# Block-sparse attention and an expert router on one core: masks multiplied on GpSimd in some units, sums read from PSUM, squares on ScalarE, ranks in 16 bits, one branch at the end

## The chip, the cores and the metric

The kernel runs on one core of a Trainium2 chip. The core has five engines with a queue each: TensorE (PE in the profile, its weight loads PEld), VectorE (DVE), ScalarE (ACT), GpSimd (POOL) and SyncE (SP), which issues most of the transfers. The metric is the device time of one execution in microseconds (us).

## The reference, cut to what matters

Four batches of eight heads attend over 768 tokens with a mask of 32 x 32 blocks: a block sees its neighbours, the first and the last block, and three blocks drawn at random. The result, 3072 rows of 512, goes to a router that sends each row to the one of eight experts whose embedding it is closest to in angle, and the expert's two matmuls are scaled by the gate.

```python
# attention: q, k, v are (4, 8, 768, 64)
scores = scale * np.matmul(q, k.transpose(0, 1, 3, 2))
mask = np.abs(blk_i - blk_j) <= 1
mask = mask | (blk_i == 0) | (blk_j == 0) | (blk_i == n_blocks - 1) | (blk_j == n_blocks - 1)
for qb in range(n_blocks):
    for kb in sampled_blocks[qb]:
        mask[qb * block:(qb + 1) * block, kb * block:(kb + 1) * block] = True
scores = np.where(mask, scores, -1000000000.0)
attn = np.exp(scores - np.max(scores, axis=-1, keepdims=True))
attn = attn / (np.sum(attn, axis=-1, keepdims=True) + 1e-09)
attn_out = np.matmul(attn, v)
x = attn_out.transpose(0, 2, 1, 3).reshape(3072, 512)
# router: w1 is (8, 512, 1024), w2 is (8, 1024, 512)
xn = x / (np.linalg.norm(x, axis=-1, keepdims=True) + 1e-06)
en = expert_emb / (np.linalg.norm(expert_emb, axis=-1, keepdims=True) + 1e-06)
logits = xn @ en.T / tau
expert_idx = np.argmax(logits, axis=1)
probs = np.exp(logits - logits.max(-1, keepdims=True))
probs /= probs.sum(-1, keepdims=True) + 1e-09
gate_w = probs[np.arange(N), expert_idx]
for e in range(E):
    mask = expert_idx == e
    h = np.maximum(x[mask] @ w1[e], 0.0)
    out[mask] = gate_w[mask, None] * (h @ w2[e])
```

## The kernel before

The attention is cut into 16 pairs of heads (g), each pair into two halves of 384 queries (qh, a half has the number w), each half into six units of 128 keys (kc): 192 units, numbered u. For a unit, score_fast adds the mask and the scores up in PSUM (both heads and both halves of the keys side by side, 64 x 64 each, so four matmuls for the mask and four for the scores) and ScalarE takes the exponential. Masked places get a large negative number from the mask's matmul, a product of two 16-bit tables of blocks, so that the exponential is zero.

```python
def score_fast(k, u):

    nc = k.nc
    g, qh, kc = u // (2 * NC), u // NC % 2, u % NC
    kt, qt = k.turned[g]
    ps = k.big.tile([P, 2, 512], F32, name="sc", tag="big")
    queries = slice(qh * HALF, (qh + 1) * HALF)
    quarters = [(h, r, slice(kc * P + D * r, kc * P + D * (r + 1))) for r in range(2) for h in range(2)]
    for rows, cols, first in ((k.kmask, k.qmask, True), (kt, qt, False)):
        for h, r, keys in quarters:
            nc.tensor.matmul(ps[D * r:D * (r + 1), h, 0:HALF], lhsT=rows[D * h:D * (h + 1), keys],
                             rhs=cols[D * h:D * (h + 1), queries], start=first, stop=not first)
    e = k.ep.tile([P, 2, HALF], F32, name="e", tag="e")
    k.exps = nc.scalar.activation(e, ps[:, :, 0:HALF], ACT.Exp, scale=SCALE)
    k.es[u] = e


def attend_fast(k, u):
    nc = k.nc
    g, qh, kc = u // (2 * NC), u // NC % 2, u % NC
    e, v = k.es[u], k.loaded[g][2]
    if kc == 0:
        k.av = k.acc.tile([P, 2, 512], F32, name="av", tag="av")
        k.first = e
    elif kc == 1:
        k.esum = k.sp.tile([P, 2, HALF], F32, name="esum", tag="esum")
        with k.tc.issue_after(k.summed.ins if u > NC else k.exps.ins):
            k.summed = nc.vector.tensor_tensor(out=k.esum, in0=k.first, in1=e, op=ALU.add)
    else:
        k.summed = nc.vector.tensor_tensor(out=k.esum, in0=k.esum, in1=e, op=ALU.add)
    for r in range(2):
        for h in range(2):
            nc.tensor.matmul(k.av[D * h:D * (h + 1), r, 0:HALF], lhsT=v[D * r:D * (r + 1), h, kc, :],
                             rhs=e[D * r:D * (r + 1), h, :], start=(kc == 0), stop=(kc == NC - 1))
    if kc == NC - 1:
        part = k.sp.tile([P, HALF], F32, name="part", tag="part")
        nc.scalar.copy(out=part, in_=k.av[:, 1, 0:HALF])
        at = k.sp.tile([P, HALF], F32, name="at", tag="at")
        k.summed = nc.vector.tensor_tensor(out=at, in0=k.av[:, 0, 0:HALF], in1=part, op=ALU.add)
        k.done[u // NC] = (at, k.esum)
```

At the end of a half, settle turns the result back into rows, sums the exponentials of each row with matmuls by ones, and divides. The squares of the rows (for the router's norm) are taken on GpSimd, and those of the last half on ScalarE.

```python
    # settle(k, w): at is turned back into PSUM (rows) by matmuls, and then
    for t in range(NQ):
        for h in range(2):
            for r in range(2):
                for s in range(2):
                    cols = slice(t * P + D * s, t * P + D * (s + 1))
                    nc.tensor.matmul(sums[D * s:D * (s + 1), t, h, r:r + 1], lhsT=esum[D * r:D * (r + 1), h, cols],
                                     rhs=k.ones[D * r:D * (r + 1), 0:1], start=True, stop=True)
    den = k.dens[:, w, :]
    nc.vector.reduce_sum(out=den.rearrange("p (t h) -> p t h", t=NQ), in_=sums, axis=AX.X)
    nc.vector.tensor_scalar(out=den, in0=den, scalar1=1e-9, scalar2=None, op0=ALU.add)
    # ... (1 / den times rows gives x, and the partial logits, both on VectorE)


def squares(k, w):

    nc = k.nc
    b, j, qh = w // (2 * NPAIR), w // 2 % NPAIR, w % 2
    chunks = slice(qh * NQ, (qh + 1) * NQ)
    x = k.x[b][:, chunks, j, 0:P]
    sq = k.sp.tile([P, NQ, P], F32, name="sq", tag="sq", bufs=1)
    nc.gpsimd.tensor_tensor(out=sq, in0=x, in1=x, op=ALU.mult)
    width = P // 2
    while width:
        out = sq[:, :, 0:width] if width > 1 else k.nsq[b][:, chunks, j:j + 1]
        k.squared = nc.gpsimd.tensor_tensor(out=out, in0=sq[:, :, 0:width], in1=sq[:, :, width:2 * width],
                                            op=ALU.add).ins
        width //= 2
```

The loop over the units, in which scores run two units ahead of attend:

```python
    for u in range(units):
        # ...
        if u % NC == 3 and NC < u < units - 2 * NC:
            settle(n, u // NC - 1)
        if u % NC == 4 and NC < u < units - 2 * NC:
            squares(n, u // NC - 1)
        # ... (routing, ranks and early dispatch of a finished batch, by a plan)
        steps = [partial(attend_fast, n, u)] + ([partial(score_fast, n, u + 2)] if u + 2 < units else [])
        for step in reversed(steps) if u % NC == 0 else steps:
            step()
        # ... (the next pair's keys and queries are turned in units 0 and 1 of a pair)
```

The rank of a row in its expert, by triangular and full matrices of ones (k.before, k.ones, fp32):

```python
    oh = k.oh[:, b * NC:(b + 1) * NC, :]
    ps = two_banks(k, "rk")[:, 0]
    rk = ps[:, 0:NC * E].rearrange("p (c e) -> p c e", e=E)
    nc.tensor.matmul(rk, lhsT=k.before, rhs=oh, start=True, stop=False)
    nc.tensor.matmul(rk, lhsT=k.ones, rhs=k.seen[:, b * NC:(b + 1) * NC, :], start=False, stop=True)
    nc.tensor.matmul(ps[:, NC * E:(NC + 1) * E], lhsT=k.ones, rhs=k.seen[:, (b + 1) * NC, :], start=True, stop=True)
```

The expert tiles have 128 rows of one expert. Five (NE) are made from the first two batches while attention still runs, the later ones when all rows are known. Late tiles number NL = 24 at most, of which NU = 19 are always run and the others if k.used, the number that the routing asks for, is larger. Weights are fetched up to two tiles ahead into three sets of buffers, rows two tiles ahead, and the rows of the next tile are turned (prepare) before the second matmul of the tile before it.

```python
def fetch(k, i):

    if i + 2 < NE + NL and i + 2 != NE:
        fetch_rows(k, i + 2)
    need = [(t, at) for t in range(NE + NL) for at in parts(t)]
    begin = [t for t, _ in need].index(i)
    for t, at in need[k.loads:begin + 3]:
        for _ in fetch_weights(k, t, at):
            pass


def expert_tile(k, i, meanwhile=None, then=None):
    # ... hp: two halves of 4 x 4 matmuls by w1, relu into h, then
    if i + 1 < NE + NL:
        prepare(k, i + 1)
    # ... yp: 8 matmuls by w2; finish: y = gate * yp on VectorE, scattered to the output by GpSimd


# end of expert_tiles
    for i in range(NE + NU):
        if i + 2 == NE:
            for _ in between:
                pass
        fetch(n, i)
        # ... (expert_tile, or mixed_tile for two halves of 64 rows of two experts)
    used = n.nc.values_load(n.used[0:1, 0:1], min_val=0, max_val=NL)
    with ExitStack() as more:
        for i in range(NU, NL):
            more.enter_context(n.tc.If(used > i))
            n.scattered = None
            fetch(n, NE + i)
            expert_tile(n, NE + i)
```

Rows of late tiles come from memory by four indirect transfers that GpSimd issues, and VectorE turns them (from fetch_rows and prepare, cut):

```python
            for g in range(NG):
                k.nc.gpsimd.indirect_dma_start(
                    out=x[:, g], out_offset=None, in_=quarters,
                    in_offset=bass.IndirectOffsetOnAxis(ap=k.quarter[:, g, t:t + 1], axis=0),
                    bounds_check=quarters.shape[0] - 1, oob_is_err=False,
                )
# ...
    with k.tc.issue_after(k.relu):
        nc.vector.transpose(out=turned.rearrange("p d (g t) -> p d g t", g=NG),
                            in_=x[:, :, 0:P].rearrange("p g (t d) -> p d g t", d=ND))
```

At the very end a second branch asks whether all row sums were in a safe range (count_good); if not, exact computes everything again with the row's maximum taken off first.

```python
    fast(n)
    good = n.nc.values_load(n.good[0:1, 0:1], min_val=0, max_val=N * H)
    with tc.If(good < N * H):
        exact(n)
```

## Time and profile before

| | |
|---|---|
| time, median of 3 | 699.31 us (699.29 to 699.33) |
| span of the profiled execution | 697.6 us |
| exponentials on ScalarE, 192 | 155.5 us, 810 ns each |
| matmuls of scores, 1536 records | 164.4 us busy |
| matmuls of attend, 1536 records | 160.7 us busy |
| mask matmuls, 768 | 73.7 us busy, 323 ns each |
| additions of exponentials on VectorE, 128 and 32 | 128.8 and 31.1 us |
| squares on GpSimd, 31 and 217 instructions | 28.5 us and some 114 us |
| memory read and written | 147.66 and 16.07 MB |

Matmuls overlap: the time of one record is from its start to its end, and several are under way at once, so a stage is read from the distances between starts. A group's busy time is the union of its records. In a list in order of time, records of one kind that follow each other are merged, with their number behind an x; in brackets stands how long the engine had been idle and what ended that.

### The profile page before, as it was taken

Reading aid. Unit: us, or ns where it says so; the run is one execution under the profiler, and the core shown is the slowest. Engines: PE = TensorE matmul, PEld = TensorE weight load, DVE = VectorE, ACT = ScalarE, POOL = GpSimd, SP = SyncE. Lnnn points to the kernel's source line nnn. Section 1 sums busy time; section 2 is a strip of 40 time slices with the busy share of each in tenths; the row PEclk is TensorE's granted clock in tenths of the full one; section 3 lists DMA queues with packets and bytes.
Section 4 is the critical chain, followed back from the end, with each engine's and each line's share of the span. In section 5 each row is a group of like instructions: output and inputs, shape, how many; then the busy total and the mean of one; then the engine's idle time right before and its main releaser. Section 6 shows DMA issues by size and latency. Waiting matters only on the chain.

```text
span 697.6 us, 19415 instructions
## 1 busy us (share of the span) xinstructions
PE 682.9 (98%) x8237; PEld 453.5 (65%) x8237; DVE 344.4 (49%) x733; ACT 188.4 (27%) x266; POOL 295.6 (42%) x450
## 2 busy tenths in 40 slices
PE   9999999999999999999999999999999999999992
PEld 4677777555555557557767677666576755667770
DVE  6887778777788888765671111211121111211120
ACT  5555555555555555553100000000100000000000
POOL 1355466544774468545402244323342243323430
PEclk9999999999999999999999999999999999999997
DMA  7733444575226769652999889998899998999990
GB/s 123 130 62 50 55 70 70 130 145 118 55 43 161 138 160 195 222 172 94 341 406 369 339 303 341 357 350 302 297 409 403 405 372 310 420 390 419 359 342 25
DMA packets 172650, 164.87 MB, mean 236 GB/s; under 512 B 129340, under 2 KB 129340, under 8 KB 169478
## 3 DMA queue, kind: packets, MB, share of 16 engines
q1 hardware_dynamic: 165734, 149.86, 68.0%
q0 software_dynamic: 5216, 13.43, 5.3%
q8 instruction: 68, 1.11, 0.7%
q10 hardware_dynamic: 1600, 0.20, 0.2%
q14 instruction: 32, 0.26, 0.1%
HBM read 147.66 MB, written 16.07 MB: 235 GB/s over the span
## 4 chain that ended last, share of the span: by engine, by line
PE 96%; DMA 1%; issue 1%; DVE 0%; POOL 0%; ACT 0%; POOLq 0%
PE hp L896 23%; PE sc L368 22%; PE yp L911 22%; PE av L390 18%; PE back L425 3%; PE hp L939 2%; PE yp L959 2%; PE back L418 2%; DMA out_dram<-y,slot_l 1%; PE warm L81 1%; PE xg_ps L872 0%; DVE row L945 0%; PE hp L951 0%; PE rk L569 0%; POOL out_dram L920 0%
## 5 line engine op out<-in xcount | busy, mean ns | idle before, releaser
L371 ACT ACTIVATE e<-sc 128x768 f32<-128x768 f32 x192 | 155.5, 810 | 149.6 <-PE sc L368 147.7
L896 PEld LDWEIGHTS hp<-xgt,w 128*128 128x128 f32 x1472 | 167.8, 192 | 10.8 <-issue 10.2
L896 PE MATMUL hp<-xgt,w 128*128 128x128 f32 x1472 | 169.3, 275 | 0.0
L368 PE MATMUL sc<-qt,kt 64*64 64x384 f32 x1536 | 164.4, 482 | 0.0
L911 PE MATMUL yp<-w,h 128*128 128x512 f32 x368 | 161.7, 592 | 0.0
L390 PE MATMUL av<-e,vld 64*64 64x384 f32 x1536 | 160.7, 486 | 0.0
L387 DVE TENSOR_TENSOR esum<-esum,e 128x768 f32<-128x768 f32 x128 | 128.8, 1006 | 34.7 <-ACT e L371 30.9
L911 PEld LDWEIGHTS yp<-w,h 128*128 128x128 f32 x368 | 68.2, 190 | 77.0 <-issue 76.5
L453 POOL TENSOR_TENSOR sq<-sq 128x192 f32<-128x192 f32 (+1 forms) x186 | 101.8, 547 | 13.9
L817 POOL DMA_INDIRECT xg<-x_dram,quarter x88 | 88.3, 1004 | 32.9 <-issue 27.7
L390 PEld LDWEIGHTS av<-e,vld 64*64 64x64 f32 x1536 | 64.1, 133 | 46.0 <-issue 17.4
L899 ACT ACTIVATE h<-hp 128x512 f32<-128x512 f32 x23 | 13.7, 597 | 291.4 <-PE hp L896 291.4
L368 PEld LDWEIGHTS sc<-qt,kt 64*64 64x64 f32 x1536 | 66.9, 133 | 31.3 <-issue 23.2
L920 POOL DMA_INDIRECT out_dram<-y,slot_l x20 | 20.1, 1007 | 156.4 <-DVE y L919 151.1
L903 DVE TENSOR_SCALAR h<-hp 128x512 f32<-128x512 f32 x23 | 15.9, 691 | 129.4 <-PE hp L896 129.4
L449 POOL TENSOR_TENSOR sq<-x 128x384 f32<-128x384 f32 x31 | 28.5, 918 | 116.7 <-DVE part L438 97.9
L368 PE MATMUL sc<-qmask,kmask 64*64 64x384 bf16 x768 | 73.7, 323 | 0.1
L919 DVE TENSOR_SCALAR y<-yp,gate 128x512 f32<-128x512 f32 x20 | 15.0, 751 | 100.9 <-PE yp L911 88.8
L368 PEld LDWEIGHTS <-kmask 64*64 64x64 bf16 x768 | 31.4, 107 | 26.3 <-issue 21.4
L385 DVE TENSOR_TENSOR esum<-e 128x768 f32<-128x768 f32 x32 | 31.1, 973 | 7.5 <-ACT e L371 7.5
L425 PE MATMUL back<-ones,esum 64*64 64x1 f32 x1536 | 27.5, 191 | 0.0
L425 PEld LDWEIGHTS back<-ones,esum 64*64 64x64 f32 x1536 | 26.7, 135 | 0.0
(204 smaller groups left out, 367.5 us busy)
## 6 DMA issues: line engine op xcount, KB each, us to landing
w<-in_moe_w_dram SPq DMA_DIRECT2D x54, 2048.0 KB
w<-in_moe_w_dram SPq DMA_DIRECT2D x16, 512.0 KB
x_dram<-x SPq DMA_DIRECT2D x24, 258.0 KB
vld<-in_v_dram SPq DMA_DIRECT2D x32, 192.0 KB
kld<-in_k_dram SPq DMA_DIRECT2D x60, 96.0 KB
qld<-in_q_dram SPq DMA_DIRECT2D x60, 96.0 KB
x_early<-x SPq DMA_DIRECT2D x12, 258.0 KB
xg<-x_dram,quarter POOLq DMA_INDIRECT x88, 6.2
```

The costliest lines, as they stand in the source:

```text
L368: nc.tensor.matmul(ps[D * r:D * (r + 1), h, 0:HALF], lhsT=rows[D * h:D * (h + 1), keys], rhs=cols[D * h:D * (h + 1), queries], start=first ...
L371: k.exps = nc.scalar.activation(e, ps[:, :, 0:HALF], ACT.Exp, scale=SCALE)
L385: k.summed = nc.vector.tensor_tensor(out=k.esum, in0=k.first, in1=e, op=ALU.add)
L387: k.summed = nc.vector.tensor_tensor(out=k.esum, in0=k.esum, in1=e, op=ALU.add)
L390: nc.tensor.matmul(k.av[D * h:D * (h + 1), r, 0:HALF], lhsT=v[D * r:D * (r + 1), h, kc, :], rhs=e[D * r:D * (r + 1), h, :], start=(kc == 0 ...
L425: nc.tensor.matmul(sums[D * s:D * (s + 1), t, h, r:r + 1], lhsT=esum[D * r:D * (r + 1), h, cols], rhs=k.ones[D * r:D * (r + 1), 0:1], star ...
L449: nc.gpsimd.tensor_tensor(out=sq, in0=x, in1=x, op=ALU.mult)
L453: k.squared = nc.gpsimd.tensor_tensor(out=out, in0=sq[:, :, 0:width], in1=sq[:, :, width:2 * width], op=ALU.add).ins
L817: k.nc.gpsimd.indirect_dma_start(out=x[:, g], out_offset=None, in_=quarters, in_offset=bass.IndirectOffsetOnAxis(ap=k.quarter[:, g, t:t + ...
L896: nc.tensor.matmul(hp[:, f, :], lhsT=w1[:, d, (f0 + f) * P:(f0 + f + 1) * P], rhs=xt[:, d, :], start=(d == 0), stop=(d == ND - 1))
L911: nc.tensor.matmul(yp, lhsT=h[:, f, :], rhs=w2[:, f, :], start=(f == 0), stop=(f == NF - 1))
L920: k.scattered = nc.gpsimd.indirect_dma_start(out=k.out[:, :], out_offset=bass.IndirectOffsetOnAxis(ap=slot, axis=0), in_=y[:, :], in_offse ...
```

## The change

Six things, meant to take work off the engine that is busiest and off the end:

- In the second and the fifth unit of a half (CUT, kc 1 and 4), other than in the first pair and a few units of each batch (WHOLE), the mask is no longer added by matmuls. build_cut makes the mask of those keys once, as ones and zeros in 16 bits, and GpSimd multiplies the exponentials by it. So that there is time for it, scores run three units ahead instead of two, with five buffers of exponentials instead of four.
- The two parts of each row sum are read from PSUM by two instructions in place of a reduction and an addition.
- The squares of all halves go to ScalarE.
- k.oh, k.seen and the matrices of ones for the ranks are in 16 bits, and two of the three rank matmuls become one.
- Rows and weights are fetched ahead, and rows turned ahead, only for tiles below k.stop. That is NE + NU in the main part, and in a conditional tile the tile itself.
- The conditional tiles and the exact path lie behind one common branch, on k.todo, which counts whether a row sum is out of range and whether k.used is over NU. A conditional tile fetches its own rows and weights and turns its rows inside its block.

```diff
@@ -51,6 +51,12 @@
 
+AHEAD = 3
+CUT = (1, 4)
+
+WHOLE = {1: (10, 19), 2: (10, 19), 3: (10, 13, 19)}
+
+
 class Net:
# ...
@@ -363,13 +371,33 @@
     quarters = [(h, r, slice(kc * P + D * r, kc * P + D * (r + 1))) for r in range(2) for h in range(2)]
-    for rows, cols, first in ((k.kmask, k.qmask, True), (kt, qt, False)):
+    cut = g > 0 and kc in CUT and u % (2 * NC * NPAIR) not in WHOLE.get(g // NPAIR, ())
+    for rows, cols, first in ((k.kmask, k.qmask, True), (kt, qt, False))[int(cut):]:
         for h, r, keys in quarters:
             nc.tensor.matmul(ps[D * r:D * (r + 1), h, 0:HALF], lhsT=rows[D * h:D * (h + 1), keys],
-                             rhs=cols[D * h:D * (h + 1), queries], start=first, stop=not first)
+                             rhs=cols[D * h:D * (h + 1), queries], start=first or cut, stop=not first)
     e = k.ep.tile([P, 2, HALF], F32, name="e", tag="e")
     k.exps = nc.scalar.activation(e, ps[:, :, 0:HALF], ACT.Exp, scale=SCALE)
+    if cut:
+        mask = k.cut[:, CUT.index(kc), queries].unsqueeze(1).broadcast_to([P, 2, HALF])
+        k.squared = nc.gpsimd.tensor_tensor(out=e, in0=e, in1=mask, op=ALU.mult).ins
     k.es[u] = e
+
+
+def build_cut(k, i):
+
+    nc = k.nc
+    if i == 0:
+        k.cut = k.const.tile([P, len(CUT), S], BF16, name="cut")
+    ps = two_banks(k, "cut_ps")
+    for h in range(2):
+        for r in range(2):
+            rows = slice(D * h, D * (h + 1))
+            nc.tensor.matmul(ps[D * r:D * (r + 1), h, 0:HALF],
+                             lhsT=k.kmask[rows, CUT[i] * P + D * r:CUT[i] * P + D * (r + 1)],
+                             rhs=k.qmask[rows, h * HALF:(h + 1) * HALF], start=True, stop=True)
+    nc.scalar.activation(k.cut[:, i].rearrange("p (h t) -> p h t", h=2), ps[:, :, 0:HALF], ACT.Relu, bias=1.0,
+                         scale=-10.0 / NEG)
 
# ...
@@ -425,8 +453,10 @@
     den = k.dens[:, w, :]
-    nc.vector.reduce_sum(out=den.rearrange("p (t h) -> p t h", t=NQ), in_=sums, axis=AX.X)
-    nc.vector.tensor_scalar(out=den, in0=den, scalar1=1e-9, scalar2=None, op0=ALU.add)
+
+    per_row = den.rearrange("p (t h) -> p t h", t=NQ)
+    nc.vector.tensor_scalar(out=per_row, in0=sums[:, :, :, 0], scalar1=1e-9, scalar2=None, op0=ALU.add)
+    nc.vector.tensor_tensor(out=per_row, in0=sums[:, :, :, 1], in1=per_row, op=ALU.add)
 
# ...
@@ -441,25 +471,9 @@
 
# ... (the version on GpSimd goes out here)
-def last_squares(k, w):
-
     b, j, qh = w // (2 * NPAIR), w // 2 % NPAIR, w % 2
     for c in range(qh * NQ, (qh + 1) * NQ):
-        sq = k.sp.tile([P, P], F32, name="sq_l", tag="sq_l")
+        sq = k.sp.tile([P, P], F32, name="sq", tag="sq")
         k.nc.scalar.activation(sq, k.x[b][:, c, j, 0:P], ACT.Square,
# ...
@@ -480,6 +494,13 @@
     nc.vector.tensor_copy(out=k.good, in_=ps[:, 0:1])
+
+    bad = k.dp.tile([P, 1], F32, name="bad")
+    nc.vector.tensor_scalar(out=bad, in0=ps[:, 0:1], scalar1=float(N * H), scalar2=None, op0=ALU.is_lt)
+    tiles = k.dp.tile([P, 1], F32, name="tiles")
+    nc.vector.tensor_scalar(out=tiles, in0=k.used, scalar1=float(NU), scalar2=None, op0=ALU.is_gt)
+    k.todo = k.const.tile([P, 1], I32, name="todo")
+    nc.vector.tensor_tensor(out=k.todo, in0=bad, in1=tiles, op=ALU.add)
 
# ...
@@ -566,9 +587,10 @@
     rk = ps[:, 0:NC * E].rearrange("p (c e) -> p c e", e=E)
-    nc.tensor.matmul(rk, lhsT=k.before, rhs=oh, start=True, stop=False)
-    nc.tensor.matmul(rk, lhsT=k.ones, rhs=k.seen[:, b * NC:(b + 1) * NC, :], start=False, stop=True)
-    nc.tensor.matmul(ps[:, NC * E:(NC + 1) * E], lhsT=k.ones, rhs=k.seen[:, (b + 1) * NC, :], start=True, stop=True)
+
+    nc.tensor.matmul(ps[:, 0:(NC + 1) * E].rearrange("p (c e) -> p c e", e=E), lhsT=k.ones_b,
+                     rhs=k.seen[:, b * NC:(b + 1) * NC + 1, :], start=True, stop=False)
+    nc.tensor.matmul(rk, lhsT=k.before, rhs=oh, start=False, stop=True)
     k.count = k.rp.tile([P, E], F32, name="count")
# ...
@@ -849,9 +871,9 @@
 
-    if i + 2 < NE + NL and i + 2 != NE:
+    if i + 2 < k.stop and i + 2 != NE:
         fetch_rows(k, i + 2)
-    need = [(t, at) for t in range(NE + NL) for at in parts(t)]
+    need = [(t, at) for t in range(k.stop) for at in parts(t)]
     begin = [t for t, _ in need].index(i)
# ...
@@ -983,7 +1005,7 @@
     n.acc, n.big = pool("acc", 1, space=PSUM), pool("big_f", 2, space=PSUM)
-    n.ld, n.tp, n.ep = pool("ld", 3), pool("tp", 2), pool("ep", 4)
+    n.ld, n.tp, n.ep = pool("ld", 3), pool("tp", 2), pool("ep", 5)
     pairs = B * NPAIR
# ...
@@ -1012,15 +1034,15 @@
     load_pair(n, 1, (2,))
-    plan, experts = [], build_experts(n)
+    plan, experts, ahead = [], build_experts(n), 2
     for u in range(units):
             settle(n, u // NC - 1)
-        if u % NC == 4 and NC < u < units - 2 * NC:
-            squares(n, u // NC - 1)
+        if u in (3, 5):
+            build_cut(n, u // 2 - 1)
         if u in (2, 4, 7):
# ...
@@ -1030,12 +1052,18 @@
             if when == u % (per * NPAIR):
-                with n.tc.issue_after(n.summed.ins), n.tc.issue_after(n.exps.ins), n.tc.issue_after(n.tick.ins):
+                with n.tc.issue_after(n.summed.ins), n.tc.issue_after(n.exps.ins), n.tc.issue_after(n.tick.ins), \
+                        n.tc.issue_after(n.squared):
                     what()
 
-        steps = [partial(attend_fast, n, u)] + ([partial(score_fast, n, u + 2)] if u + 2 < units else [])
+        scored = u + (AHEAD if u > NC else 2)
+        steps = [partial(attend_fast, n, u)] + [partial(score_fast, n, i) for i in range(ahead, min(scored + 1, units))]
+        ahead = scored + 1
         for step in reversed(steps) if u % NC == 0 else steps:
             step()
+        if u % NC == 5 and NC < u < units - 2 * NC:
+            with n.tc.issue_after(n.exps.ins):
+                squares(n, u // NC - 1)
         turn = u % per - (0 if g else NC - 1)
# ...
@@ -1101,12 +1129,21 @@
         next(between, None)
+
+
+def last_tiles(n):
+
     used = n.nc.values_load(n.used[0:1, 0:1], min_val=0, max_val=NL)
             more.enter_context(n.tc.If(used > i))
-            n.scattered = None
-            fetch(n, NE + i)
+            n.scattered = n.relu = None
+            n.stop = NE + i + 1
+            fetch_rows(n, NE + i)
+            for at in parts(NE + i):
+                for _ in fetch_weights(n, NE + i, at):
+                    pass
+            prepare(n, NE + i)
             expert_tile(n, NE + i)
# ...
@@ -1143,6 +1180,21 @@
         expert_tiles(n, between(), last_rows, last_route, lambda: next(n.late))
+
+
+def more(n):
+
+    n.rings, n.loads = {}, 0
+    with ExitStack() as ctx:
+        def pool(name, bufs, **kw):
+            return ctx.enter_context(n.tc.tile_pool(name=name, bufs=bufs, **kw))
+
+        n.wp, n.wp2 = pool("wp_l", 1), pool("wp2_l", 1)
+        n.eps, n.hps = pool("eps_l", 1, space=PSUM), pool("hps_l", 1, space=PSUM)
+        last_tiles(n)
+    good = n.nc.values_load(n.good[0:1, 0:1], min_val=0, max_val=N * H)
+    with n.tc.If(good < N * H):
+        exact(n)
 
# ...
@@ -1201,9 +1254,9 @@
     fast(n)
-    good = n.nc.values_load(n.good[0:1, 0:1], min_val=0, max_val=N * H)
-    with tc.If(good < N * H):
-        exact(n)
+    todo = n.nc.values_load(n.todo[0:1, 0:1], min_val=0, max_val=2)
+    with tc.If(todo > 0):
+        more(n)
 
 # ---- launch: one core; inputs and outputs as the reference has them ----
```

## The prediction

> **What bounds the kernel now.** I read the page first (busy shares, then the chain that ended last), then one stretch of the attention stage in order of time, then the last 40 us.
>
> ```profile
> PE 682.9 (98%) x8237; PEld 453.5 (65%) x8237; DVE 344.4 (49%) x733; ACT 188.4 (27%) x266; POOL 295.6 (42%) x450
> ```
>
> TensorE is busy for 98% of the span and the chain is 96% PE: whatever does not take work off PE, or does not make PE wait, moves nothing. The attention stage takes the first 320 us or so, the expert tiles the rest.
>
> Attention in order of time (start us, duration us, engine, line):
>
> ```profile
> 202.72 0.34 PE L368 MATMUL sc<-qmask,kmask 64*64 64x384 bf16 x4
> 202.88 0.82 PE L368 MATMUL sc<-qt,kt 64*64 64x384 f32 x8
> ...
> 203.53 0.82 PE L390 MATMUL av<-e,vld 64*64 64x384 f32 x8
> ...
> 204.17 0.34 PE L368 MATMUL sc<-qmask,kmask 64*64 64x384 bf16 x4
> ...
> 204.33 0.82 PE L368 MATMUL sc<-qt,kt 64*64 64x384 f32 x8
> ...
> 204.67 1.23 DVE L387 TENSOR_TENSOR esum<-esum,e 128x768 f32<-128x768 f32 x1 [0.38 <-ACT e L371]
> ```
>
> Read the starts, since the ends overlap. Mask to scores 0.16 us, scores to attend 0.65, attend to the next mask 0.64: a unit is 1.45 us, of which the mask is 0.16. (The page's mean of 323 ns for a mask matmul is a latency of four that run at once.) There is no gap between units: PE's issue is the bound. Six units plus the turning back of one half (settle, about 1.25 us from 200.68 to 202.0) give some 9.9 us a half; successive squares on GpSimd, at 125.02, 134.84, 144.63 and 154.62, show 9.8.
>
> The end:
>
> ```profile
> 663.86 6.88 PE yp L911 x16
> 670.74 0.03 issue
> 670.77 0.76 DVE y L919
> ```
>
> ```profile
> 671.80 1.01 POOL L920 DMA_INDIRECT out_dram<-y,slot_l  x1 [7.77 <-DVE y L919]
> 675.53 1.03 POOL L817 DMA_INDIRECT xg<-x_dram,quarter  x1 [2.73 <-issue]
> 676.87 1.00 POOL L817 DMA_INDIRECT xg<-x_dram,quarter  x1 [0.30 <-issue]
> 678.17 1.00 POOL L817 DMA_INDIRECT xg<-x_dram,quarter  x1 [0.30 <-DMA out_dram<-y,slot_l]
> 679.47 1.00 POOL L817 DMA_INDIRECT xg<-x_dram,quarter  x1 [0.30 <-issue]
> 685.81 1.01 POOL L920 DMA_INDIRECT out_dram<-y,slot_l  x1 [5.34 <-DVEq L1105]
> ```
>
> The page of transfers has 20 scatters with slot_l, but NU is 19: the last tile of this run lies inside the first conditional block. Working the routing out from the reference on its inputs also gives used = 20. PE goes through the branch without a gap: hp follows yp at 670.74, because rows, weights and the turned rows of that tile had been prepared while the tiles before it ran. GpSimd, however, needs 2.73 us instead of 0.30 between scatter and gather there; that is what the branch costs an engine.
>
> [...]
>
> ```profile
> 164.21 0.83 POOL L449 TENSOR_TENSOR sq<-x 128x384 f32<-128x384 f32 x1 [4.13 <-DVE part L438]
> 164.59 1.26 DVE L387 TENSOR_TENSOR esum<-esum,e 128x768 f32<-128x768 f32 x1 [0.41 <-ACT e L371]
> 165.11 1.19 POOL L453 TENSOR_TENSOR sq<-sq 128x192 f32<-128x192 f32 x1
> ```
>
> The add takes 1.26 us where it takes about 0.95 by itself: it begins to move at 165.04, when GpSimd is done, and GpSimd's next instruction (0.60 us in an undisturbed place) takes 1.19[...]. [...]the trace's 0.83 us for 384 elements and 0.19 us for three make 1.68 ns an element, so 1.48 us. I take 1.6. [...]the first eight warm-up matmuls take 3.59 us, 0.45 each, the same matmuls later are quicker.
>
> **The change part by part.**
>
> *Masks.* A cut unit drops four mask matmuls, 0.16 us of PE. Pair 0 is left whole, so 15 pairs x 2 halves x 2 units = 60, less the seven in WHOLE: 53 units, of which 26 are second units of a half and 27 fifth ones. 53 x 0.16 = **8.5 us off** PE. Two build_cut calls put back 2 x 0.16, with a weight load, +0.4.
>
> *What takes their place.* The chain of a cut unit is scores, exp, GpSimd's product, attend. From the end of the scores' issue: 0.24 us to exp's start (204.98 to 205.22), 0.81 exp, 0.09 to GpSimd, 1.6 product, 0.1 to PE: 2.84 us. AHEAD = 3 gives it the PE work in between. For the fifth unit that is attend 0.64, scores 0.81, settle 1.25, attend 0.64, scores 0.81 = 4.1 us: enough. For the second unit it is attend, scores, scores, attend = 2.9 us: just enough[...]: after settle VectorE has 1.3 us of small work and then three adds of 0.95 for units 3 to 5, so it ends them about 4.2 us after settle's last matmul; the product becomes ready 3.9 us after that matmul and waits for the third add, some 0.5 us. The same three adds are followed by the addition that frees av, which attend of the next half needs; that chain (about 5.0 us from settle's end) is equal to PE's own time (5.0). So I put a wait of 0 to 0.5 us at each of the 26 second units and take the middle: 26 x 0.25 = **6.5 us on**.
>
> *Squares to ScalarE.* 31 x 3 activations of 0.30 plus 0.19 for reading the sum: 1.46 us a half. With six exps (4.86) and the copy (0.47) ScalarE has 6.8 of 9.8 us; they stand behind the exp of a third unit, ahead of a fourth, which is not cut and has 3 us to spare. Off the path, 0. GpSimd loses about 4.5 us a half of squares and gains 3.2 of products. *Row sums from PSUM:* one reduce and one add become two small instructions, about 0.3 us either way: 0.
>
> *Ranks in 16 bits.* Three fp32 matmuls with 0.19 us weight loads take PE from 119.48 to 120.25, 0.77 us. Two bf16 matmuls with 0.1 us loads take an estimated 0.25. 4 x 0.5 = **2.0 us off**.
>
> *The branch at the end.* k.stop ends prefetching at NU, and the conditional tile now fetches its own rows inside the branch. As used is 20, todo is 1 and the branch is taken. GpSimd gathers only after its own scatter of tile 23, which waits for y. Counted from the end of yp (670.74 before): scatter done +2.1; branch 2.7, perhaps twice since todo and used are both read; four gathers 1.3 apart, so the last starts at +8.7; the shortest landing of such a gather in the last 100 us is 3.0, so +11.7; turning on VectorE 1.1 and two hand-overs, +13. Weights can be earlier: SyncE reads the branch for itself, long before.[...] A second branch would add up to 2.7. Before, hp began at +0. **About 15 us on.** Not loading the two unused sets of weights (8.4 MB) saves nothing, since those transfers lie beside PE.
>
> Sum: 699.3 - 8.5 + 0.4 + 6.5 - 2.0 + 15 = 710.7; I say 710.5.
>
> **The rivals.** (A) The masks come off cleanly and only the last tile costs: no waits at second units, 699.3 - 10.1 + 15 = 704. For it: the WHOLE list leaves out units where GpSimd has routing work, so that somebody looked after that engine[...]. (B) [...]an add waits 1.6 us, av is freed late, and PE waits 1 us a half: 30 us on instead of 6.5, 730 at the worst; 717 at half of it. Against it: VectorE had 80% in this stage with GpSimd's squares beside it and PE had no gaps. (C) The end costs little, because gathers in an idle memory land in less than 3 us and the branch is read ahead: +8 instead of 15, 704 with the waits and 697 without. (D) The weights of the last tile, too, wait for the branch or for their memory: 4.2 MB at the 383 GB/s of the last stretch are 11 us; beside the gathers that adds perhaps 5: 716. What was meant, no cost at the end and all masks gained, would give 689; the trace speaks against it, since the conditional tile does run.
>
> **Range and chances.** The end is the largest term and I hold 8 to 20 for it; the waits are 0 to 15. Together 698 to 721. Faster by over 2% needs less than 685.3, under what even a free end would give: 0.04. Slower by over 2% needs more than 713.3, some 3 us above my centre: 0.33. Within 2%: 0.63.
>
> **What would show it.** In the changed profile: mask matmuls 768 less 212 = 556; PE gaps of 0.2 to 0.5 us before attend of second units, put down to GpSimd's product, and none at fifth ones; products of 1.6 us alone and up to 2.5[...]; half periods near 9.7. At the end a PE gap of about 13 us between the yp of the last tile but one and the hp of the last, ended by VectorE's turn, with gathers ahead of it, and slow first matmuls. A gap under 6 us, or waits over 1 us in each half, would make the prediction wrong.

## The result, and the profile after

The changed kernel takes 728.81 us (727.69 to 729.40) where the kernel before takes 699.3 us on the same chip: 1.042 times as long, with an interval of 1.0408 to 1.0435. The prediction was 710.5 us with a range of 698 to 721. The profiled spans are 727.7 and 697.6 us, so 30.1 us have to be found.

The page of the changed kernel: busy times, the shares of the chain that ended last, and groups (busy us, mean ns of one | idle us of the engine before them, and what ended most of it).

```profile
PE 678.0 (93%) x8017; PEld 420.2 (58%) x8017; DVE 353.3 (49%) x734; ACT 213.7 (29%) x454; POOL 246.2 (34%) x247
...
PE 48%; issue 4%; DMA 1%; POOL 0%; DVE 0%; ACT 0%; POOLq 0%
...
L418 PE MATMUL av<-e,vld 64*64 64x384 f32 x1536 | 155.3, 489 | 7.3 <-DVE at L424 5.8
...
L415 DVE TENSOR_TENSOR esum<-esum,e 128x768 f32<-128x768 f32 x128 | 137.5, 1074 | 29.3 <-POOL e L383 18.7
L383 POOL TENSOR_TENSOR e<-e,cut 128x768 f32<-128x768 f32 x53 | 93.1, 1756 | 170.1 <-ACT e L380 88.0
...
L377 PE MATMUL sc<-qmask,kmask 64*64 64x384 bf16 x556 | 47.7, 323 | 0.2
```

TensorE has 4.9 us less to do, and its share has gone from 98% to 93%: 50 us of the span are now without PE, where it had been 15. The 212 mask matmuls are gone. Attend, which never waited before, has waited 7.3 us, and 5.8 of them for VectorE (at, the addition that ends a half), not for the product on GpSimd. VectorE's additions of exponentials have grown from 1006 to 1074 ns.

The end of the changed kernel in order of time (start us, duration us):

```profile
672.53 0.97 POOL L942 DMA_INDIRECT out_dram<-y,slot_l  x1 [13.03 <-DVE y L941]
674.98 1.05 POOL L839 DMA_INDIRECT xg<-x_dram,quarter  x1 [1.48 <-issue]
...
678.95 1.00 POOL L839 DMA_INDIRECT xg<-x_dram,quarter  x1 [0.30 <-issue]
...
685.67 1.08 DVE L899 STREAM_TRANSPOSE xgt<-xg 128x512 f32<-128x512 f32 x1 [13.42 <-DMA xg<-x_dram,quarter]
...
686.86 9.97 PE L918 MATMUL hp<-xgt,w 128*128 128x128 f32 x64 [15.40 <-DVE own L902]
...
696.67 7.03 PE L933 MATMUL yp<-w,h 128*128 128x512 f32 x16
...
704.77 1.02 POOL L942 DMA_INDIRECT out_dram<-y,slot_l  x1 [24.83 <-DVEq L1137]
```

The chain of work that ended last, in order of time, over the same stretch:

```profile
664.59 6.88 PE yp L933 x16
...
681.17 23.37 issue
```

Three things are to be seen. PE stands still for 15.40 us, in order: scatter, branch, gathers, landing, turn. The first matmuls of the tile take 9.81 us from start to start of the second ones (686.86 to 696.67) instead of 7.14. And the last matmul ends at 703.70, but the span only at 727.69: the way out, from the last PE work to the end, is 24.0 us, and was 12.85 (684.74 to 697.59). Here the chain stops helping: its 23.37 us of "issue" are time for which it names no work, and what happens after the last scatter is no part of it. What ends last are instructions of GpSimd's sequencer, which don't count as busy. Asked for by their lines (minimum, median and maximum in ns, first and last start in us), in the kernel before:

```profile
L1105 POOLq INC_SWDGE_SEM  x1: 420/420/420, 689.3 to 689.3; - x1
...
L1205 POOLq INC_SWDGE_SEM  x1: 410/410/410, 695.3 to 695.3; - x1
...
L1234 POOLq DRAIN  x3: 46/107/1055, 695.7 to 697.3; - x3
```

and in the changed kernel:

```profile
L1137 POOLq INC_SWDGE_SEM  x1: 2379/2379/2379, 708.6 to 708.6; - x1
...
L1196 POOLq INC_SWDGE_SEM  x1: 2366/2366/2366, 714.9 to 714.9; - x1
...
L1287 POOLq DRAIN  x3: 46/107/9058, 717.4 to 727.4; - x3
```

By their lines, an INC_SWDGE_SEM stands in both kernels at the end of a block behind a branch, and the DRAIN at the end of the program. They have grown by 1.96, 1.96 and 8.00 us, 11.9 together; the rest of the way out is 0.8 us shorter. So the account is: the yp of tile 23 ends at 671.46 instead of 670.73, +0.7; the gap 15.4; the slow matmuls 2.7; the way out 11.1; together 29.9 of the 30.1. The first is small, the next two are what was predicted, and the last was in no sum.

### The profile page after: what moved, and what is told of

Same layout as the page of the kernel before. It is cut to its first block, busy times and chain, and to the rows that moved or that the text cites. A ratio compares the mean times of both kernels' runs of the same rounds, so it can differ in the third digit from the quotient of the medians.

```text
span 727.7 us, 19031 instructions
## 1 busy us (share of the span) xinstructions
PE 678.0 (93%) x8017; PEld 420.2 (58%) x8017; DVE 353.3 (49%) x734; ACT 213.7 (29%) x454; POOL 246.2 (34%) x247
## 3 DMA queue, kind: packets, MB, share of 16 engines
q0 software_dynamic: 4960, 12.90, 4.8%
## 4 chain that ended last, share of the span: by engine, by line
PE 48%; issue 4%; DMA 1%; POOL 0%; DVE 0%; ACT 0%; POOLq 0%
PE hp L918 22%; PE yp L933 21%; PE yp L981 2%; PE hp L961 2%; DMA out_dram<-y,slot_l 1%; PE hp L973 0%; PE xg_ps L894 0%; POOL e L383 0%; PE av L418 0%; PE back L453 0%; POOL out_dram L942 0%; PE back L446 0%; PE quarter_ps L697 0%; DVE y L941 0%; PE slot_ps L680 0%
## 5 line engine op out<-in xcount | busy, mean ns | idle before, releaser
L918 PE MATMUL hp<-xgt,w 128*128 128x128 f32 x1472 | 172.0, 278 | 15.4 <-DVE own L902 15.4
L377 PE MATMUL sc<-qt,kt 64*64 64x384 f32 x1536 | 157.9, 482 | 0.0
L415 DVE TENSOR_TENSOR esum<-esum,e 128x768 f32<-128x768 f32 x128 | 137.5, 1074 | 29.3 <-POOL e L383 18.7
L383 POOL TENSOR_TENSOR e<-e,cut 128x768 f32<-128x768 f32 x53 | 93.1, 1756 | 170.1 <-ACT e L380 88.0
L418 PEld LDWEIGHTS av<-e,vld 64*64 64x64 f32 x1536 | 52.1, 133 | 66.8 <-issue 33.6
L839 POOL DMA_INDIRECT xg<-x_dram,quarter x80 | 80.3, 1004 | 29.2 <-issue 24.3
L377 PEld LDWEIGHTS sc<-qt,kt 64*64 64x64 f32 x1536 | 58.9, 133 | 45.5 <-issue 43.7
L377 PE MATMUL sc<-qmask,kmask 64*64 64x384 bf16 x556 | 47.7, 323 | 0.2
L477 ACT ACTIVATE sq<-x 128x128 f32<-128x128 f32 x96 | 28.3, 300 | 13.3 <-DVE x L465 13.3
L377 PEld LDWEIGHTS <-kmask 64*64 64x64 bf16 x556 | 18.0, 107 | 24.5 <-issue 24.5
L899 DVE STREAM_TRANSPOSE xgt<-xg 128x512 f32<-128x512 f32 x20 | 21.8, 1092 | 13.4 <-DMA xg<-x_dram,quarter 13.4
```

What stands on the lines that cost most here:

```text
L383: k.squared = nc.gpsimd.tensor_tensor(out=e, in0=e, in1=mask, op=ALU.mult).ins
L477: k.nc.scalar.activation(sq, k.x[b][:, c, j, 0:P], ACT.Square, accum_out=k.nsq[b][:, c, j:j + 1])
L839: k.nc.gpsimd.indirect_dma_start(out=x[:, g], out_offset=None, in_=quarters, in_offset=bass.IndirectOffsetOnAxis(ap=k.quarter[:, g, t:t + ...
L918: nc.tensor.matmul(hp[:, f, :], lhsT=w1[:, d, (f0 + f) * P:(f0 + f + 1) * P], rhs=xt[:, d, :], start=(d == 0), stop=(d == ND - 1))
```

## The experiments

The prediction's theory (the tile is cold) says that the way out is long because a tile ran behind the branch, or because the branches are nested. Its rivals say that the way out follows something else that the change took away with the prefetching: GpSimd stands idle before the end, or it has issued fewer indirect transfers. In the attention stage, the dispute is whether the products pay for the masks. All kernels compute the whole result; where one issues extra gathers, they go to buffers that nobody reads. Ratios are to the kernel before on the same chip. "Transfers" are GpSimd's indirect transfers: 110 in the changed kernel, 118 in the kernel before, which also gathers rows (four transfers a tile) for two tiles that never run. The page's queue of these transfers shows the same eight as 4960 packets against 5216, 32 each. Every gather that the runs add or take away has 32 packets, so they don't tell the number of transfers from the number of packets.

| run | us | ratio (interval) | transfers | way out us | DRAIN us |
|---|---|---|---|---|---|
| before | 699.3 | 1 | 118 | 12.85 | 1.055 |
| changed | 728.81 | 1.042 (1.0408 to 1.0435) | 110 | 23.99 | 9.058 |
| e1_all_main | 704.27 | 1.0076 (1.0059 to 1.0093) | 110 | 16.97 | 9.061 |
| e3_attention_only | 698.66 | 0.9995 (0.9986 to 1.0004) | 118 | 11.28 | 1.055 |
| e4_end_only | 727.09 | 1.0405 (1.0387 to 1.0422) | 110 | 23.67 | 9.058 |
| e5_warm_tile | 710.29 | 1.0164 (1.0147 to 1.0180) | 110 | 23.98 | 9.058 |
| e6_not_nested | 728.77 | 1.0422 (1.0404 to 1.0439) | 110 | 24.11 | 9.058 |
| x1_busy_gpsimd | 703.43 | 1.0059 (1.0042 to 1.0076) | 110 | 17.27 | 9.061 |
| x2_gathers_kept | 693.66 | 0.9919 (0.9902 to 0.9935) | 118 | 7.34 | 1.057 |
| x3_gathers_early | 695.12 | 0.9940 (0.9924 to 0.9957) | 118 | 9.28 | 1.057 |
| b1_units_3_and_4 | 715.11 | 1.0238 (1.0224 to 1.0252) | 118 | 6.97 | 1.057 |
| b2_masks_on_pe | 691.08 | 0.9884 (0.9869 to 0.9899) | 118 | 7.00 | 1.057 |
| b3_four_more | 694.76 | 0.9937 (0.9919 to 0.9956) | 114 | 8.21 | 0.731 |
| b4_sixteen_early | 695.03 | 0.9941 (0.9923 to 0.9959) | 126 | 7.87 | 1.711 |
| c1_changed_four_more | 715.93 | 1.0238 (1.0221 to 1.0255) | 114 | 12.57 | 0.733 |
| c2_before_eight_fewer | 709.41 | 1.0144 (1.0127 to 1.0161) | 110 | 22.89 | 9.056 |
| c3_fifth_unit_alone | 694.37 | 0.9926 (0.9910 to 0.9943) | 118 | 7.07 | 1.057 |
| c4_two_more | 703.68 | 1.0061 (1.0041 to 1.0082) | 112 | 17.21 | 9.224 |

### Which part of the change costs

**e3_attention_only**: the kernel before with every part of the change but those at the end (the branch, k.todo, k.stop).

> The kernel before with everything of the change but the end: masks, row sums, squares, ranks, and the old prefetch and branches. Theory A: the last tile but one ended 0.7 us later in the changed kernel than before, so 699.3 + 0.7 = 700.0. Theory B: 710 or more.

**e4_end_only**: the kernel before with only those at the end. The core of it, as in the change:

```diff
-    if i + 2 < NE + NL and i + 2 != NE:
+    if i + 2 < k.stop and i + 2 != NE:
...
+    todo = n.nc.values_load(n.todo[0:1, 0:1], min_val=0, max_val=2)
+    with tc.If(todo > 0):
+        more(n)
```

> The kernel before with nothing of the change but the end: k.stop, the conditional tile that fetches for itself, the common branch. Theory A: 699.3 + 29 = 728. Theory B: about 714.

Measured: 698.66 and 727.09 us. The attention side nets nothing that can be told from zero, and the end alone loses 28.1 us (together 27.8, where the whole change loses 29.5). In e4 the gap is 14.60 us, and the DRAIN the same 9.058 us.

**e1_all_main**: the changed kernel with 20 late tiles in the main part, so that the last tile is prepared like the others and the branch isn't taken.

```diff
-NU = N // G - NE
+NU = N // G - NE + 1
```

> The changed kernel with NU = 20, so that all 20 late tiles of these inputs stand in the main part and the branch is not taken. Theory A (the loss is the conditional tile: 15.4 us of standing PE, 2.7 us of slow matmuls and 11 us of a longer way out): 728.8 - 18 - 11 = 700, or a few us less if skipping everything by one branch is shorter than the way out before. Theory B (GpSimd's products hold VectorE up and attention carries half of the loss): not under 714.

704.27 us, 4 more than theory A's 700. PE has no cold tile and ends at 685.44, but the way out is 17 us, with the long DRAIN:

```profile
L1287 POOLq DRAIN  x3: 40/107/9061, 692.5 to 702.1; - x3
```

So the long DRAIN doesn't come from a tile behind the branch. **e6_not_nested** puts the test for the exact path behind the common branch instead of in it:

```diff
# in more(n)
-    good = n.nc.values_load(n.good[0:1, 0:1], min_val=0, max_val=N * H)
-    with n.tc.If(good < N * H):
-        exact(n)
# after the common branch
+    good = n.nc.values_load(n.good[0:1, 0:1], min_val=0, max_val=N * H)
+    with tc.If(good < N * H):
+        exact(n)
```

> The changed kernel with the test of the row sums and the exact path taken out of the common branch and set behind it, as before; the conditional tile is as cold as in the changed kernel. If the 11 us of the way out come from the exact path lying inside the branch that is taken: 728.8 - 11 = 718. If they come from the conditional tile itself or from the idle time ahead of it: 728, no change.

728.77 us: how the branches are nested is worth nothing. **e5_warm_tile** keeps the tile behind the branch, but fetches its rows and weights and turns its rows in the main part (with the exact path outside, as in e6; shown in part):

```diff
-    between, n.scattered, n.stop = iter(between), None, NE + NU
+    between, n.scattered, n.stop = iter(between), None, NE + NU + (0 if n.exact else 1)
...
-            fetch_rows(n, NE + i)
+            if i > NU or n.exact:
+                fetch_rows(n, NE + i)
```

> The changed kernel with the rows, weights and turned rows of the one conditional tile prepared ahead in the main part, inside the common branch only its matmuls, and the test of the row sums behind that branch. If the standing PE and its slow clock are 18 us of the loss: 728.8 - 18 = 710.7, with the long way out (2.4 and 9.1 us) kept. If the branch itself holds PE up: 715 or more.

710.29 us, 18.5 us less than the changed kernel: this is the cold tile, shown by itself (15.4 of gap and 2.7 of slow matmuls in the profile). The way out stays at 23.98 us.

### What makes the way out long

**x1_busy_gpsimd** gives GpSimd a memset and twelve multiplications, written at the start of the last tile of e1 and meant to run during it.

```diff
+    if i == NE + NU - 1 and not k.exact:
+        busy = ring(k, "row0", 0, 1, k.wp2, [P, NF // 2 * P])
+        nc.gpsimd.memset(busy, 1.0)
+        for _ in range(12):
+            nc.gpsimd.tensor_tensor(out=busy[:, 0:384], in0=busy[:, 0:384], in1=busy[:, 0:384], op=ALU.mult)
```

> The run with all 20 late tiles in the main part (704.3 us), and GpSimd kept at work through the last tile by a fill and twelve products of 128x384 in a spare buffer (some 10 us, beside PE). On the way out GpSimd there took 2.39 us to raise the semaphores of what was skipped and 9.06 us to drain, against 0.42 and 1.06 in the kernel before. If a GpSimd that stood idle for long before the last scatter is the cause: 0.42 and 1.06 again, 704.3 - 10 = 694. If the number or the nearness of its indirect transfers is: unchanged, 704.

703.43 us, with a DRAIN of 9.061 us. But this run did not do what it was meant to do. Its trace has the twelve products at 579.1 to 589.9 us, long before the last tile, and GpSimd stands idle ahead of the last scatter as it did in e1:

```profile
685.62 0.97 POOL L947 DMA_INDIRECT out_dram<-y,slot_l  x1 [13.02 <-DVE y L946]
```

So x1 says nothing about an idle GpSimd; the run after the next one does. **x2_gathers_kept** is e1 with the gathers for the two tiles that never run, as the kernel before has them:

```diff
-    if i + 2 < k.stop and i + 2 != NE:
+    if i + 2 < k.stop + (0 if k.exact else 2) and i + 2 != NE:
```

> The run with all 20 late tiles in the main part (704.3 us), and the eight gathers of rows for two tiles that do not run put back, as the old prefetch had them (not their weights). If the gathers, by their number or by coming shortly before the last scatter, are what made the way out quick: 0.42 and 1.06 us, 694. If idle time of GpSimd is the cause: they come in the last two tiles as well, so also 694. If something else in the branch is: 704.

693.66 us, 10.6 less than e1, by doing eight useless gathers more:

```profile
L1287 POOLq DRAIN  x3: 40/107/1057, 690.1 to 692.0; - x3
```

**x3_gathers_early** issues eight such gathers instead that are written five tiles ahead of the last one (in its trace they run at 578.5 to 588.7 us):

```diff
+    if i == NE + 14 and not k.exact:
+        quarters = k.x_dram.rearrange("n (e w) -> (n e) w", e=ND)
+        for j in range(2 * NG):
+            spare = ring(k, f"row{4 * (j % 2)}", 0, 1, k.wp2, [P, NF // 2 * P])
+            # ... (one indirect gather from quarters into spare)
```

> The run with all 20 late tiles in the main part (704.3 us), and eight more gathers some five tiles before the end, into spare buffers, so that GpSimd issues as many transfers as the kernel before but stands idle in the last tile as in the changed kernel. If their number decides[...]: 694. If being idle shortly before the end decides: 704.

695.12 us and 1.057 us of DRAIN, although GpSimd is as idle ahead of the last scatter as in e1 and x1:

```profile
685.20 0.98 POOL L952 DMA_INDIRECT out_dram<-y,slot_l  x1 [13.03 <-DVE y L951]
```

So an idle GpSimd isn't the cause, and it is not how near to the end the gathers are, but how many there have been. Is it then "the more, the quicker"? **b3_four_more** (x2 with one tile ahead instead of two), **b4_sixteen_early** (x3 with 4 * NG gathers) and **c4_two_more** (x3 with NG // 2, that is two) change the number alone.

> As the quick run with the gathers kept, but with the four gathers of one more tile instead of eight: 114 indirect transfers, between the 110 of the slow way out and the 118 of the quick one. If being under some number is what makes it slow: either of the two, 2.4 and 9.1 us or 0.42 and 1.06, nothing between; if the cost grows with what is missing: some 1.4 and 5.

> As the run with eight early gathers, but with sixteen: 126 indirect transfers. If the quick way out needs at least some number between 110 and 118: 0.42 and 1.06 us.[...]

> The run with all 20 late tiles in the main part and two more gathers, 112 indirect transfers. The drains so far are 0.0815 us times a count that stands at 111, 9, 13 and 21 for 110, 114, 118 and 126 transfers. If the count starts again after about 112: 0.57 us (7), or 9.2 us (113) if it has not yet done so at 112.

The DRAIN takes 0.731, 1.711 and 9.224 us for 114, 126 and 112 transfers: for b3 and b4 none of the outcomes named ahead, for c4 the second. In these runs it grows by 0.082 us a transfer (from 114 to 126: 0.98 / 12; from 110 to 112: 0.163 / 2), and between 112 and 114 it falls from 9.224 to 0.731 us. INC_SWDGE_SEM falls, too: it takes 2.379 and 2.366 us in the changed kernel (110), 0.340 in the run c1 below (114) and 0.420 and 0.410 in the kernel before (118), which makes 0.020 us a transfer from 114 to 118. No run shows why.

Then the same must hold in the two kernels that the case is about. **c1_changed_four_more** is the changed kernel itself with four early gathers (the edit of x3 with NG in place of 2 * NG), **c2_before_eight_fewer** the kernel before without the eight (the core of its edit):

```diff
-    if i + 2 < NE + NL and i + 2 != NE:
+    if i + 2 < NE + (NL if k.exact else NU + 1) and i + 2 != NE:
...
-    if i + 1 < NE + NL:
+    if i + 1 < NE + NL and i + 1 in k.rows:
```

> The changed kernel itself, cold conditional tile and all, with four more gathers into spare buffers some five tiles before the end: 114 indirect transfers. If the number of transfers is the cause of the long way out: drain 0.7 instead of 9.06, and 728.8 - 10 = 718.5. If the number matters only where no conditional tile runs: 728.8.

> The kernel before without the eight gathers (and the turning) of rows for tiles that do not run: 110 indirect transfers, all else as it was. If the number is the cause: drain 9.06, the semaphores 2.4, so 699.0 + 8 + 2 = 709. If not: 699.

Both went over to the other side. The changed kernel with four gathers more takes 715.93 us, 12.9 less, and keeps its cold tile (a PE gap of 14.53 us). Between the two profiles lie 14.1 us; 11.4 of them are the way out, and the rest is PE, which ends 2.7 us earlier:

```profile
L1147 POOLq INC_SWDGE_SEM  x1: 340/340/340, 706.3 to 706.3; - x1
...
L1297 POOLq DRAIN  x3: 40/107/733, 712.0 to 713.3; - x3
```

The kernel before with eight fewer takes 709.41 us, 10.1 more, with a way out that is 10.0 longer:

```profile
L1238 POOLq DRAIN  x3: 46/107/9056, 696.8 to 706.4; - x3
```

### What the products on GpSimd are worth

**b2_masks_on_pe** is x2 with every mask on TensorE again; all else of the change stays.

```diff
-    cut = g > 0 and kc in CUT and u % (2 * NC * NPAIR) not in WHOLE.get(g // NPAIR, ())
+    cut = False
```

> The quick run with the gathers kept (693.7 us), with no unit cut: all masks by matmuls again, no product on GpSimd, all the rest of the change as it is. If the masks' gain (53 x 0.16 = 8.5 us) is paid back by PE's waits for products and the additions behind them (some 7 us more than without): 693.7 + 8.5 - 7 = 695. If the waits come from the squares on ScalarE or from scores running three ahead: 702.

691.08 us, which is less than x2 (693.66), less than the kernel before by 8.2 us (5.9 of them in the way out) and the fastest of all these. The cut masks cost 2.6 us instead of gaining 2. The two are told apart by when the rows of the first and of the last half are turned back. b2:

```profile
L446 PE MATMUL back<-back,at x768: 222/223/273, 24.5 to 327.8; 64*64 64x72 f32 x192
```

x2, with the masks cut:

```profile
L446 PE MATMUL back<-back,at x768: 222/223/273, 24.5 to 329.9; 64*64 64x72 f32 x192
```

That is 2.1 us between the two ends (303.0 against 305.0 from first to last half). In between, b2 has 9.79 us from the first attend of a half to that of the next, in all halves without routing. In x2 most take 9.46 to 9.55, so the masks do bring about 0.3 us a half; but five halves take 0.77 to 1.14 us longer than in b2. Up to the last half, gains (5.5 us) and losses (5.5) are equal, and the last half loses 2.0, in two waits:

```profile
319.23 0.63 PE L894 MATMUL first<-ident,xg 128*128 128x128 f32 x4 [0.78 <-PE sc L377]
323.25 0.88 PE L418 MATMUL av<-e,vld 64*64 64x384 f32 x8 [1.14 <-POOL e L383]
```

The second is a wait for the product of a fifth unit itself. The first is put down to PE's own scores, which had been done; what it waited for isn't named.

What a good half and a bad one look like is seen in the changed kernel. A good one, around the product of its second unit:

```profile
124.97 0.82 PE L418 MATMUL av<-e,vld 64*64 64x384 f32 x8
...
125.78 0.82 PE L377 MATMUL sc<-qt,kt 64*64 64x384 f32 x8
...
126.10 1.66 POOL L383 TENSOR_TENSOR e<-e,cut 128x768 f32<-128x768 f32 x1 [3.87 <-ACT e L380]
...
126.58 0.82 PE L377 MATMUL sc<-qt,kt 64*64 64x384 f32 x8
...
127.23 1.47 PE L418 MATMUL av<-e,vld 64*64 64x384 f32 x16
```

The product of the second unit lies beside scores, and the attends of the first and second unit follow each other without a gap. A bad one:

```profile
109.60 1.78 POOL L383 TENSOR_TENSOR e<-e,cut 128x768 f32<-128x768 f32 x1 [2.60 <-ACT e L380]
...
109.97 2.22 DVE L415 TENSOR_TENSOR esum<-esum,e 128x768 f32<-128x768 f32 x1
...
113.53 0.21 DVE L562 TENSOR_TENSOR oh<-pick,mx 128x48 bf16<-128x48 f32 x1
113.66 2.01 DVE L415 TENSOR_TENSOR esum<-esum,e 128x768 f32<-128x768 f32 x2
...
116.80 0.55 DVE L424 TENSOR_TENSOR at<-av,part 128x384 f32<-128x384 f32 x1
...
117.40 1.52 PE L418 MATMUL av<-e,vld 64*64 64x384 f32 x16 [1.12 <-DVE at L424]
```

The product of the fifth unit runs until 111.38, and the addition that began beside it at 109.97 ends 0.82 us after that: 2.22 us instead of 0.95. That is no single case. Of the 13 additions of exponentials in the changed kernel that began while a product was running, twelve ended 0.81 to 0.82 us after the product's end (the last began 0.05 us ahead of it and ended 0.90 after it). The other way about, the 24 products that began while an addition was running all ended 1.50 to 1.52 us after the addition's end. In b2, without products, all 128 additions at L415 take 0.915 to 0.992 us. So in these traces the one that began later ended a nearly fixed time after the other. From there on VectorE has no pause up to 116.80: the routing of the batch, two more additions, the divisions, and only then at, which frees av. PE waits 1.12 us for it. Where VectorE has no routing in a half, it makes the 1.3 us good and nothing is seen. In x2 all five halves that lose have 1.6 to 3.0 us of routing work on VectorE; one with 3.4 us of it loses nothing, so the place of that work counts, too.

**b1_units_3_and_4** moves the products to the fourth and fifth unit (with one unit left whole in each of three batches, so that 57 are cut), away from the second unit, where the prediction had put the waits. **c3_fifth_unit_alone** cuts the fifth only.

```diff
# b1
-CUT = (1, 4)
+CUT = (3, 4)
-WHOLE = {1: (10, 19), 2: (10, 19), 3: (10, 13, 19)}
+WHOLE = {1: (10,), 2: (10,), 3: (10,)}
# c3
-    cut = g > 0 and kc in CUT and u % (2 * NC * NPAIR) not in WHOLE.get(g // NPAIR, ())
+    cut = g > 0 and kc == CUT[1] and u % (2 * NC * NPAIR) not in WHOLE.get(g // NPAIR, ())
```

> The quick run with the gathers kept (693.7 us), with the fourth and fifth unit of a half cut (kc 3 and 4) instead of the second and fifth, 57 units in all. Both have 4 to 5 us of PE work between scores and attend, and no product lies ahead of the three additions of units 3 to 5 that av waits for, other than those of 3 and 4 themselves. If the some 7 us of standing PE come from the product of a second unit being near the half's end: 693.7 - 7 - 0.6 = 686. If they come from VectorE having too much to do in those halves in any case, or if two products one behind the other hold its additions up: 693 or more.

> The quick run with the gathers kept, with only the fifth units cut (27). The run with all masks on PE took 691.1. If the second unit's product, near the end of a half, is what makes PE wait: 691.1 - 27 x 0.16 = 686.8. If any product costs more than its mask, by delaying VectorE: 691 or more.

b1 takes 715.11 us, 21.5 more than x2, and all of it in the attention stage:

```profile
L446 PE MATMUL back<-back,at x768: 222/223/273, 23.8 to 351.3; 64*64 64x72 f32 x192
```

PE's waits for at (us in all, times, the longest) are, first in x2, then in b1:

```profile
PE av L418 <- DVE at L424: 5.7, 6, 1.2
```

```profile
PE av L418 <- DVE at L424: 19.3, 16, 2.1
```

Two products in a row delay two additions in a row (in the half at 263.33 us, two products took 4.22 us and the two additions beside them 3.46), just ahead of the end of the half. c3 takes 694.37 us, 3.3 more than b2: without a single product in a second unit, the halves with routing still lose about as much as in x2 (10.92 us where b2 has 9.79). A half without routing, with one unit cut, takes 9.63 us, so a mask taken out is worth the 0.16 us of the prediction; the last half loses 0.9. The interval of c3 touches that of x2, so this does not order the two; it does show that the second unit was not the main place.

## Why the prediction was wrong, point by point

**The end, the failed step.** "The branch at the end" counts from the end of yp to the start of the next hp, some 13 us, says "About 15 us on" and stops there. It takes the way out after the last matmul to be as before, but for "A second branch would add up to 2.7". The way out grew by 11.1 us. The reason was in the part of the change that the sum left at nothing: it asked what the prefetching for unused tiles saves in weights ("saves nothing") and didn't ask about the eight gathers that go with them. Without them the program has 110 transfers on GpSimd instead of 118, and INC_SWDGE_SEM and DRAIN take 11.9 us more. c1 (a way out 11.4 us shorter by four more) and c2 (10.0 us longer by eight fewer) show it in both kernels. Nothing in the profile before tells that it would come: its own DRAIN of 1.055 us is an unremarkable line.

**The cold tile.** Mechanism right, size 3 us short. The gap was 15.4 instead of 13: the last gather began 7.5 us after yp's end rather than the 8.7 of the sum, but it was 6.7 us from there to the turn, not the shortest landing of 3.0. "Weights can be earlier" did not hold: SyncE had passed the common branch at 629.9, but its fetch waited for the y of tile 23, and the weights were issued at 672.38, 0.9 us after yp's end. Up to some 686 the tile's own 4.2 MB came in beside the gathers (stretch, its length, busy of the five engines, clock, DMA share, GB/s):

```profile
676.00:680.00 4.00, 0.00 (x0) 0.00 (x0) 0.00 (x0) 0.00 (x0) 3.03 (x4) 0.50 0.97 398
680.00:684.00 4.00, 0.00 (x0) 0.00 (x0) 0.00 (x0) 0.00 (x0) 0.00 (x0) 0.50 0.98 339
...
686.00:690.00 4.00, 3.14 (x15) 3.17 (x16) 0.96 (x3) 0.00 (x0) 0.00 (x0) 0.50 0.16 59
```

That is rival D's transfer, with an effect of up to 3.7 us instead of its 5. In the kernel before, the landing of 3.0 was that of the very last gather, with 90 GB/s in the 2 us from 680; the four of the tile ahead of it took 6.0 to 7.6. No run had the gathers of the cold tile alone, so how much of the 3.7 the weights make is open. The slow first matmuls cost 2.7 us (9.81 instead of 7.14), for which the 15 us of the sum leave some 2 over the 13 of the gap. The granted clock is 1.00 up to 675.2, 0.50 from 675.3 to 692.2 and 1.00 from 692.3 on: hp runs at 0.50 for 5.4 us, with 0.21 us from start to start, and then with 0.11. (In c1, where it takes 9.20 us to the first yp, some 4.1 us at 0.50 are an estimate from these figures.)

**The masks and the waits.** 556 mask matmuls, as predicted, and 0.16 us for each, as c3's halves show. What was wrong is the waits, in size and in place. With "8.5 us off" for the masks, x2's profile, 2.0 us longer than b2's, makes the waits 10.5 us where the prediction has "6.5 us on", at "each of the 26 second units". (By halves, after netting: good ones gain 0.24 to 0.33 us each, 5.5 in all; the bad ones lose 5.5 and the last half 2.0.) At second units there is next to nothing before the last half, which loses 1.1 us less in c3; PE waits in five halves, about 1 us each, for VectorE's at, with the fifth unit's product ahead of it. The prediction had named that chain as equal to PE's own time, and then charged the neighbouring wait. Together they were to be 2.0 us off, and are 2.0 to 2.6 us on.

**Ranks, sums, squares.** Three halves take 0.61 to 0.73 us less in b2 than before (one 10.11 instead of 10.81), where the sum had 0.5 for each of four rank steps; in the first of them PE's rank matmuls, with their weights, go from 0.77 us to 0.16. Squares on ScalarE cost nothing there: halves without routing keep their 9.79 us. The first two halves take 20.62 us instead of 19.11 in b2. Half of these 1.5 us is only moved: from the second half on, scores run one unit further ahead, so that half has the scores of seven units, and the last half, from its first attend to the turning back of its rows, takes 11.19 us instead of 11.99. The other 0.75, in the half in which the masks are built, is where "+0.4" stood in the sum.

**The rivals.** A's 704 happens to be what e1 takes, for another reason. B (additions that wait for products) is what the profiles show, but it was worth at most some 10 us rather than 30; with the products placed as in b1, the kernel is 21.5 us slower still. (B's own sum was off: 30 in place of 6.5 is 734 and not 730, and half of it 719 and not 717.) C (a cheap end) fell. By terms, against 710.5: the way out +11, the cold tile +3.1, the attention side +4 (the yp of tile 23 ends 0.7 later where the sum has it 3.6 earlier). These make the 18.3 us of the miss, to half a microsecond.

## What to carry to other kernels

When a change moves or drops transfers that GpSimd issues, the end of the program belongs to the estimate: read the time from the last matmul to the end of the span and ask for the sequencer's lines in it, since here neither busy times nor the chain of work named them. Eight gathers taken out of the kernel before made that way 10.0 us longer (c2), and by how much could only be found by a run. And the products on GpSimd, well off TensorE's path, were still paid for where they held up VectorE's queue (an addition of 2.22 us instead of 0.95, then 1.12 us of PE), so look for the place where that queue has no pause left, not for the wait nearest to the product.

## What the runs showed of the hardware that was not expected

- The final DRAIN of GpSimd took 9.06 us after 110 indirect transfers, 9.22 after 112, 0.73 after 114, 1.06 after 118 and 1.71 after 126; INC_SWDGE_SEM took 2.38 us after 110 (the changed kernel), 0.34 after 114 (c1) and 0.42 after 118 (the kernel before). The kind of kernel, how near the transfers are to the end, the nesting of branches and how idle GpSimd was ahead of the last scatter made no difference to the DRAIN of over 0.005 us at one number of transfers (9.056 to 9.061 at 110, 1.055 to 1.057 at 118).
- With one common branch in place of three tests and no tile behind it, the program ended 7.0 us after the last matmul (b2) instead of 12.85, at the same DRAIN (6.97 to 9.28 us in the runs of this kind with a short DRAIN). No run changed this alone.
- A product of 128 x 768 on GpSimd took 1.65 us in the median and 1.756 in the mean. Additions of 128 x 768 on VectorE that began during one took 2.22 to 2.40 us instead of 0.95 in twelve of 13 cases and ended 0.81 to 0.82 us after it; in the kernel before, the additions that began during a square of 128 x 384, 22 in number, all ended 0.81 us after that.
